# First batch of a fused attention and gated feed-forward kernel: q/k loaded in runs of six tokens, values after the scores, alternating accumulators, and a reordered last normalization

## The chip, the cores and the metric

The kernel runs on one core of a Trainium2 chip. The metric is the device time of one execution in microseconds (us); lower is better. The first runs of the kernel before spread from 421.1 to 425.4 us, and part of the study is about why. The core has a matmul engine (PE in the profile; PEld are its weight loads), a vector engine (DVE), an activation engine (ACT), a pool engine (POOL, which here also issues most loads) and a sync engine (SP) that issues stores and transposing loads.

## The reference, cut to what matters

```python
# q, k, v: (8 batches, 8 heads, 576 tokens, 64), beacon_k/v: (8, 8, 16, 64), all float32
k_all = concat([beacon_k, k]); v_all = concat([beacon_v, v])      # 592 keys
scores = q @ k_all.T / 8;  causal mask on the 576 own keys
a = softmax(scores);  x = (a @ v_all) -> (4608 tokens, 512)
out = (gelu(x @ w_gate) * (x @ w_val)) @ w_out                    # d_ff = 1536
```

## The kernel before: the parts that the change touches

Heads are handled in four pairs per batch. For a pair, q and k are brought into the form "head dimension by token" (`qkT`), four chunks of scores are computed and put through exp, the value matmuls accumulate x and the sum z of the exponentials in PSUM, and the pair is normalized into `xT_sb`. After a batch's four pairs comes the gate/value stage (12 tiles, `gate_val`), whose output matmuls are spread over the next batch's attention. Batches 0 and 1 transpose q/k on the matmul engine, the later ones by DMA.

```python
    def load_perm(src, dst, b, h0, h1):          # batches 0 and 1: runs of 4 tokens (1 KB)
        dma(dst[:, 0:4, ...], src[b, h0:h1, 0:512, :].rearrange("h (p r) d -> p h (r d)", r=4))
        dma(dst[0:64, 4, h0:h1, :], src[b, h0:h1, 512:576, :].rearrange("h p d -> p h d"))
    ...
    def transpose_pe(b, m, pool, tag):           # 19 transposes a pair, then 4 copies on DVE
        ...
    def normalize(b, m):
        x_ps = x_of.pop(i)                       # one tile holds x and z
        act(x_sb, x_ps[:, X0 : X0 + S], ACT.Copy)
        keep(nc.vector.transpose(zT_sb, x_ps[:, Z0 : Z0 + S]))
        keep(nc.vector.reciprocal(r_sb, ...))
        keep(nc.vector.transpose(rec_sb, r_sb broadcast))
        keep(nc.vector.tensor_tensor(out=xT_sb[...], in0=x_sb, in1=rec_sb, op=ALU.mult))
    ...
    def gate_val(ci, fi, kk_late=False):         # kk_late: the matmuls that need the last pair come last
    ...
    load_qk(0)                                   # q, k of pair 0, then of the other pairs: 9 issues
    make_identity(nc, ident)                     # on the pool engine, behind those issues
    ...
    transpose_pe(0, 0, psum_s, "s")
    transpose_pe(0, 1, psum_s, "s")
    ...
        if b == 0:
            ab(0); transpose_pe(0, 2, psum_x, "x"); cd(0); transpose_pe(0, 3, psum_x, "x")
            ab(1); cd(1); ab(2); av(0); cd(2); ab(3); av(1); cd(3); av(2); av(3)
```

`ab` and `cd` are the two halves of a pair's scores, `av` its value matmuls with the normalization. (The last lines are joined here; each call stands on its own line in the kernel.) The kernel keeps every engine's instructions in program order (`keep_in_program_order`).

The softmax here doesn't subtract the row's maximum and nothing guards it: scores larger than these inputs give would overflow.

## Time and profile before

| | us |
|---|---|
| median of the first three runs | 423.2 (421.14 to 425.43) |
| span of the profiled execution | 421.2 |
| gate/value stage of batch 0 runs gapless from | 43.09 |
| one later batch, period | 43.86 |

The page of the kernel before: busy time and share of each engine, then the busy tenths of the matmul engine in 40 slices of 10.5 us.

```profile
PE 384.6 (91%) x2935; PEld 184.2 (44%) x2984; DVE 198.3 (47%) x327; ACT 207.7 (49%) x284; POOL 161.3 (38%) x282
...
PE   2476999999999999999999999999999999999996
```

The matmul engine is the busy one, and the first four slices are where it is not busy. The chain of waits (the work that ended last; columns: start, duration, what) names what holds up those slices. Kernel before, first 45 us:

```profile
6.10 7.80 DMA k_sb_93<-in_k_dram
...
13.94 0.93 PE t_ps L163 x10
...
15.45 1.03 ACT expT L155
...
33.87 0.80 DVE zT_sb L272
...
40.34 0.80 DVE zT_sb L272
...
42.28 0.77 DVE xT_sb L282
```

Scores start late because pair 1's k lands only at 13.9 us; later the chain runs through normalizations. The timeline of the matmul engine shows the idle (columns: start, duration, engine, line, operation, output and inputs, shapes, count; in brackets the idle before it and what ended it). Kernel before:

```profile
8.26 0.80 PE L163 MATMUL t_ps<-ident,q_sb_92 128*64 128x128 bf16 x9 [8.26 <-POOL ident masks.py:199]
...
34.71 0.44 PE L152 MATMUL x_ps<-expT,v_sb_94 128*64 128x496 bf16 x4 [1.17 <-DVE zT_sb L272]
...
37.94 0.44 PE L152 MATMUL x_ps<-expT,v_sb_94 128*64 128x496 bf16 x4 [1.60 <-DVE zT_sb L272]
...
43.09 0.47 PE L152 MATMUL gv_ps<-xT_sb,wg_sb 128*128 128x512 bf16 x1 [2.11 <-DVE xT_sb L282]
...
137.17 0.38 PE L152 MATMUL gv_ps<-xT_sb,wg_sb 128*128 128x512 bf16 x1 [0.61 <-DVE xT_sb L282]
```

Four things wait: the first transposes for the identity, the value steps for the only accumulator, the first gate tile for the last normalization of batch 0, and, in the last line, the first gate tile of a later batch for its last normalization. That last wait stands in each of batches 1 to 7 (0.60 or 0.61 us). The chain of waits of the kernel before just ahead of it:

```profile
133.75 0.66 ACT x_sb L155
...
134.43 0.79 DVE zT_sb L272
...
135.25 0.28 DVE r_sb L274
...
135.55 0.79 DVE rec_sb L277
...
136.36 0.77 DVE xT_sb L282
```

The copy of x (activation engine) and the transpose of z (vector engine) both read the same PSUM tile, one after the other. In this trace the two are never seen at the same time on this tile: in each of the 32 normalizations the transpose starts 0.03 us after the copy ends, and the profile names the copy as what ended its wait (here the copy ends at 134.40, the transpose starts at 134.43).

Last, the clock of the matmul engine. Columns of the stretches view: stretch, length, busy time and count per engine, then the granted clock (1.00 is full), the DMA share and GB/s. Kernel before:

```profile
42.00:44.00 2.00, 0.92 (x3) 0.40 (x3) 1.00 (x2) 0.00 (x0) 0.46 (x1) 0.81 1.25 209
44.00:46.00 2.00, 2.00 (x6) 0.70 (x5) 0.69 (x1) 0.60 (x1) 0.00 (x0) 0.50 1.28 201
46.00:48.00 2.00, 2.00 (x9) 0.80 (x8) 0.24 (x1) 0.60 (x1) 0.00 (x0) 0.84 2.22 160
```

After the 2.11 us of idle the clock is at half for 3.4 us: (1 - 0.81 + 1 - 0.50 + 1 - 0.84) x 2 / 0.5. The gate matmuls of 512 columns start 0.427 us apart in it and 0.216 us apart behind it, so eight of them take 1.7 us more.

### The profile page before, as it was taken

What the parts mean: (1) busy time and instruction counts of PE and PEld (TensorE: products, weight loads), DVE (VectorE), ACT (ScalarE), POOL (GpSimd) and SP (SyncE); (2) the same over time, 40 slices, a digit from 0 to 9 for tenths busy, and PEclk for the clock granted to TensorE, in tenths of its full rate; (3) what the DMA queues carried; (4) which work ended last, traced back from release to release, by engine and by line L of the source; (5) the groups of instructions that cost most, each with busy time, mean ns of one, the idle gap of its engine ahead of it and who ended that gap; (6) DMA issues with size and microseconds to landing.
All of it is one profiled execution on the core that took longest, in us unless ns stands there. A gap on an engine that the chain in (4) does not pass through costs nothing.

```text
span 421.2 us, 7280 instructions
## 1 busy us (share of the span) xinstructions
PE 384.6 (91%) x2935; PEld 184.2 (44%) x2984; DVE 198.3 (47%) x327; ACT 207.7 (49%) x284; POOL 161.3 (38%) x282
## 2 busy tenths in 40 slices
PE   2476999999999999999999999999999999999996
PEld 1244344444444444544454444444444444444442
DVE  0448364474337443654275426642664347443331
ACT  1365225853486338733774378436843585332210
POOL 8825481477046903591249224941410141000000
PEclk9999899999999999999999999999999999999999
DMA  7999990189914991199109941995015010000012
GB/s 82 172 206 197 173 136 3 51 74 164 100 51 48 153 137 50 31 150 159 53 26 129 143 65 51 109 160 70 26 63 89 14 51 32 21 2 25 26 50 100
DMA packets 142289, 36.23 MB, mean 86 GB/s; under 512 B 128944, under 2 KB 137648, under 8 KB 142256
## 3 DMA queue, kind: packets, MB, share of 16 engines
q0 software_dynamic: 107120, 19.15, 60.0%
q1 hardware_dynamic: 35136, 16.62, 18.8%
q8 instruction: 23, 0.38, 0.4%
q14 instruction: 10, 0.08, 0.1%
HBM read 38.27 MB, written 9.44 MB: 113 GB/s over the span
## 4 chain that ended last, share of the span: by engine, by line
PE 80%; ACT 6%; DVE 6%; issue 4%; DMA 2%; POOL 1%; ACTq 0%; POOLq 0%
PE gv_ps L152 42%; PE o_ps L152 19%; PE x_ps L152 9%; PE s_ps L152 7%; ACT expT L155 3%; ACT x_sb L155 3%; PE t_ps L163 2%; DVE zT_sb L272 2%; DMA k_sb_93<-in_k_dram 2%; DVE rec_sb L277 1%; DVE xT_sb L282 1%; POOL q_sb_92 L109 1%; DVE r_sb L274 1%; POOL k_sb_93 L109 0%; DVE qkT L178 0%
## 5 line engine op out<-in xcount | busy, mean ns | idle before, releaser
L155 ACT ACTIVATE ge_sb<-gv_ps 128x512 bf16<-128x512 f32 x108 | 64.5, 597 | 145.6 <-PE gv_ps L152 144.5
L310 DVE TENSOR_TENSOR hT_sb<-gv_ps,ge_sb 128x512 bf16<-128x512 f32 x108 | 74.7, 692 | 118.2 <-ACT ge_sb L155 118.2
L152 PE MATMUL gv_ps<-xT_sb,wg_sb 128*128 128x512 bf16 x428 | 112.8, 382 | 6.7 <-DVE xT_sb L282 6.3
L155 ACT ACTIVATE expT<-s_ps 128x1024 bf16<-128x1024 f32 (+3 forms) x128 | 103.5, 862 | 27.6 <-PE s_ps L152 25.7
L228 POOL TENSOR_SCALAR_AFFINE_SELECT expT<-expT 128x256 bf16<-128x256 bf16 (+2 forms) x140 | 53.6, 392 | 165.0 <-ACT expT L155 164.9
L152 PE MATMUL gv_ps<-xT_sb,wv_sb 128*128 128x512 bf16 x417 | 110.9, 381 | 0.7
L152 PE MATMUL o_ps<-wo_sb,hT_sb 128*128 128x512 bf16 x402 | 103.1, 380 | 3.1 <-issue 2.2
L152 PEld LDWEIGHTS <-wv_sb 128*128 128x128 bf16 x432 | 42.5, 98 | 59.2 <-issue 9.7
L152 PEld LDWEIGHTS <-wg_sb 128*128 128x128 bf16 x432 | 42.1, 98 | 50.6 <-issue 1.2
L152 PEld LDWEIGHTS <-hT_sb 128*128 128x128 bf16 x432 | 37.1, 98 | 47.3 <-issue 9.4
L152 PE MATMUL s_ps<-qkT 64*128 64x80 bf16 (+5 forms) x384 | 39.5, 294 | 6.9 <-ACT expT L155 6.6
L334 DVE COPY o_sb<-o_ps 128x512 f32<-128x512 f32 x36 | 24.8, 689 | 42.5 <-PE o_ps L152 42.5
L152 PE MATMUL x_ps<-expT,ones 128*64 128x144 bf16 (+5 forms) x576 | 43.4, 247 | 0.0
L272 DVE STREAM_TRANSPOSE zT_sb<-x_ps 128x576 f32<-128x576 f32 x32 | 25.1, 783 | 37.3 <-ACT x_sb L155 37.1
L155 ACT ACTIVATE x_sb<-x_ps 128x576 f32<-128x576 f32 x32 | 20.8, 651 | 24.9 <-issue 10.8
L152 PEld LDWEIGHTS <-qkT 64*128 64x128 bf16 x384 | 13.9, 96 | 35.4 <-issue 31.8
L152 PE MATMUL x_ps<-expT,v_sb_94 128*64 128x80 bf16 (+5 forms) x288 | 23.8, 253 | 2.9 <-DVE zT_sb L272 2.8
L282 DVE TENSOR_TENSOR xT_sb<-x_sb,rec_sb 128x576 bf16<-128x576 f32 x32 | 25.1, 784 | 1.1
L152 PEld LDWEIGHTS <-ones 128*64 128x64 bf16 (+1 forms) x576 | 23.4, 112 | 4.9 <-issue 0.2
L277 DVE STREAM_TRANSPOSE rec_sb<-r_sb 128x576 f32<-128x576 f32 x32 | 24.9, 778 | 1.1
L152 PE MATMUL x_ps<-expT,v_sb_97 128*64 128x80 bf16 (+5 forms) x288 | 22.8, 246 | 0.1
L109 POOL DMA_DIRECT2D v_sb_97<-in_v_dram x20 | 17.0, 885 | 7.6 <-DMA k_sb_96<-in_k_dram 3.8
(39 smaller groups left out, 184.4 us busy)
## 6 DMA issues: line engine op xcount, KB each, us to landing
out_dram<-o_sb SPq DMA_DIRECT2D x36, 256.0 KB, 2.0
q_sb_92<-in_q_dram POOLq DMA_DIRECT2D x13, 128.0 KB, 4.3
v_sb_94<-in_v_dram POOLq DMA_DIRECT2D x12, 128.0 KB, 7.6
wg_sb<-in_moe_w_gate_dram POOLq DMA_DIRECT2D x3, 512.0 KB, 10.6
wv_sb<-in_moe_w_val_dram POOLq DMA_DIRECT2D x3, 512.0 KB, 12.4
wo_sb<-in_moe_w_out_dram POOLq DMA_DIRECT2D x1, 1536.0 KB, 18.7
v_sb_97<-in_v_dram POOLq DMA_DIRECT2D x12, 128.0 KB, 9.8
q_sb_95<-in_q_dram POOLq DMA_DIRECT2D x12, 128.0 KB, 4.3
```

The source lines that it names most:

```text
L109: keep(nc.gpsimd.dma_start(out=out_ap, in_=in_ap))
L152: keep(nc.tensor.matmul(out_ap, lhsT, rhs, start=start, stop=stop, **kw))
L155: keep(nc.scalar.activation(out_ap, in_ap, func, **kw))
L163: keep(nc.tensor.transpose(out_ap, in_ap, ident[r0 : r0 + n, r0 : r0 + n]))
L228: nc.gpsimd.affine_select(out=d, in_=d, pattern=[[0, 2], [1, n]], compare_op=ALU.is_ge, fill=0.0, base=NB if t == 0 else 0, channel_multip ...
L272: keep(nc.vector.transpose(zT_sb, x_ps[:, Z0 : Z0 + S]))
L274: keep(nc.vector.reciprocal(r_sb, zT_sb.rearrange("p (c o) -> p c o", o=32)[:, :, 0:1]))
L277: nc.vector.transpose(rec_sb.rearrange("p (c o) -> p c o", o=32), r_sb.to_broadcast([P, S // 32, 32]))
L282: nc.vector.tensor_tensor(out=xT_sb[:, m, b * S : (b + 1) * S], in0=x_sb, in1=rec_sb, op=ALU.mult)
L310: nc.vector.tensor_tensor(out=h_of[ci][:, fi, :], in0=gv_ps[:, 1, :], in1=ge_sb, op=ALU.mult)
L334: keep(nc.vector.tensor_copy(o_sb[:, ti, :], o_ps))
```

## The change

Its intent: start the scores sooner, keep the matmul engine fed in batch 0, and shorten the hand-over to the gate stage. The diff, cut to its core:

```diff
-    def load_perm(src, dst, b, h0, h1): ...
+    def load_qk6(b, h0, h1):                    # runs of 6 tokens, 1.5 KB, no remainder
+        for w, src in enumerate((q, k)):
+            dma(qk6[b][0][0:96, w, h0:h1, :], src[b, h0:h1, :, :].rearrange("h (p r) d -> p h (r d)", r=6))
...
     def transpose_pe(b, m, pool, tag):          # 25 transposes a pair (24 of 96 columns), 2 copies
...
     def attend(b, m, t, wide=False):
+            if wide:                            # x and z in two score buffers instead of the x tile
...
     def normalize(b, m, by_act=False):
+        if by_act:                              # 1/z = exp(-ln z) on ACT, copy of x on DVE
+            act(ln_sb, z_ps, ACT.Ln)
+            keep(nc.vector.tensor_copy(x_sb, x_ps))
+            act(rec_sb, ln_sb, ACT.Exp, scale=-1.0)
+        else:
+            if m == NPAIR - 1:
+                z_first()                       # transpose of z ahead of the copy of x
+            act(x_sb, x_ps, ACT.Copy)
+            if m < NPAIR - 1:
+                z_first()
...
-    load_qk(0)
-    make_identity(nc, ident)
+    load_qk6(0, 0, 2)
+    by_diagonal(ident, ALU.not_equal, 1.0)      # identity after two issues
+    load_kb(0)
+    load_qk6(0, 2, H)
...
         if b == 0:
-            ab(0) T(2) cd(0) T(3) ab(1) cd(1) ab(2) av(0) cd(2) ab(3) av(1) cd(3) av(2) av(3)
+            ab(0) T(1) cd(0) ab(1) T(2) cd(1) ab(2) T(3) cd(2) ab(3) av(0) cd(3)
+            av(1, by_act=True)  av(2, wide=True)  av(3, by_act=True)
```

(The order lines are joined and `transpose_pe(0, n, ...)` is written T(n).) The exp buffers go from three to four. `z_first` for the last pair applies to every later batch; in batch 0 the last pair uses `by_act`.

More of the change, by code (lines that the diff above doesn't have):

```diff
@@ L6 @@
 from concourse._compat import with_exitstack
-from concourse.masks import make_identity
 P = 128
@@ L71 @@
     ring = ctx.enter_context(tc.tile_pool(name="ring", bufs=1))
-    epool = ctx.enter_context(tc.tile_pool(name="epool", bufs=3))
+    epool = ctx.enter_context(tc.tile_pool(name="epool", bufs=4))
     npool = ctx.enter_context(tc.tile_pool(name="npool", bufs=2))
@@ L81 @@
     ident = const.tile([P, P], BF16, name="ident", tag="ident")
+    nc.vector.memset(ident, 0.0)
     ones = const.tile([P, D], BF16, name="ones", tag="ones")
@@ L109, in dma, with load_kb @@
         keep(nc.gpsimd.dma_start(out=out_ap, in_=in_ap))
-    def load_perm(src, dst, b, h0, h1):
-        dma(
-            dst[:, 0:4, :, :].rearrange("p r h d -> p (r h d)").rearrange("p (h x) -> p h x", h=H)[:, h0:h1, :],
-            src[b, h0:h1, 0:512, :].rearrange("h (p r) d -> p h (r d)", r=4),
-        )
-        dma(dst[0:64, 4, h0:h1, :], src[b, h0:h1, 512:576, :].rearrange("h p d -> p h d"))
+    qk6 = {}
+    def load_qk6(b, h0, h1):
+        if b not in qk6:
+            qk6[b] = (
+                hpool.tile([P, 2, H, 6 * D], BF16, name="qk6", tag="hT_sb"),
+                npool.tile([NB, H, D], BF16, name="kb", tag="kb"),
+            )
+        for w, src in enumerate((q, k)):
+            dma(
+                qk6[b][0][0:96, w, h0:h1, :],
+                src[b, h0:h1, :, :].rearrange("h (p r) d -> p h (r d)", r=6),
+            )
+    def load_kb(b):
+        dma(qk6[b][1], beacon_k[b].rearrange("h t d -> t h d"))
     def load_keys(src, beacon, dst, b):
@@ L127, in load_qk @@
         q_sb, k_sb = q_ring[b % NRING], k_ring[b % NRING]
-        if b < NPERM:
-            for h0, h1 in ((0, 2), (2, H)) if b == 0 else ((0, H),):
-                load_perm(q, q_sb, b, h0, h1)
-                load_perm(k, k_sb, b, h0, h1)
-                if h0 == 0:
-                    dma(k_sb[64:80, 4, :, :], beacon_k[b].rearrange("h t d -> t h d"))
-        else:
-            for j in range(4):
-                dma(q_sb[:, j, :, :], q[b, :, j * P : (j + 1) * P, :].rearrange("h p d -> p h d"))
-            dma(q_sb[0:64, 4, :, :], q[b, :, 512:576, :].rearrange("h p d -> p h d"))
-            load_keys(k, beacon_k, k_sb, b)
+        for j in range(4):
+            dma(q_sb[:, j, :, :], q[b, :, j * P : (j + 1) * P, :].rearrange("h p d -> p h d"))
+        dma(q_sb[0:64, 4, :, :], q[b, :, 512:576, :].rearrange("h p d -> p h d"))
+        load_keys(k, beacon_k, k_sb, b)
     def load_v(b):
@@ L158, in transpose_pe, with tr @@
     def transpose_pe(b, m, pool, tag):
-        t_ps = pool.tile([P, 2, 1024 if tag == "s" else 1536], BF16, name="t_ps", tag=tag)
-        def tr(out_ap, in_ap, r0=0):
+        t_ps = pool.tile([P, 3 if tag == "x" else 2, 1024], BF16, name="t_ps", tag=tag)
+        qk, kb = qk6[b]
+        def tr(out_ap, in_ap):
             n = in_ap.shape[0]
-            keep(nc.tensor.transpose(out_ap, in_ap, ident[r0 : r0 + n, r0 : r0 + n]))
-        for w, src in enumerate((q_ring[b % NRING], k_ring[b % NRING])):
-            by_head = src[:, 0:4, :, :].rearrange("p r h d -> p (r h d)").rearrange(
-                "p (h r d) -> p h r d", h=H, r=4
-            )
-            base = 0 if tag == "s" else 512 * w
-            for r in range(4):
-                c = slice(r * P, (r + 1) * P)
-                for hi in range(2):
-                    tr(t_ps[64 * hi : 64 * hi + 64, w, c], by_head[:, 2 * m + hi, r, :])
-            tr(t_ps[:, w, 512:576], src[0:64, 4, 2 * m : 2 * m + 2, :])
-        tr(t_ps[:, 1, 576:592], k_ring[b % NRING][64:80, 4, 2 * m : 2 * m + 2, :], 64)
-        for w in range(2):
-            keep(
-                nc.vector.tensor_copy(
-                    qkT[:, m, w, NB : NB + 512].rearrange("p (t r) -> p t r", r=4),
-                    t_ps[:, w, 0:512].rearrange("p (r t) -> p t r", r=4),
-                )
-            )
-        keep(nc.vector.tensor_copy(qkT[:, m, :, NB + 512 : SK], t_ps[:, :, 512:576]))
-        keep(nc.vector.tensor_copy(qkT[:, m, 1, 0:NB], t_ps[:, 1, 576:592]))
+            keep(nc.tensor.transpose(out_ap, in_ap, ident[0:n, 0:n]))
+        for w in range(2):
+            for r in range(6):
+                for hi in range(2):
+                    tr(
+                        t_ps[64 * hi : 64 * hi + 64, w, r * 96 : (r + 1) * 96],
+                        qk[0:96, w, 2 * m + hi, r * D : (r + 1) * D],
+                    )
+        tr(t_ps[:, 1, S:SK], kb[:, 2 * m : 2 * m + 2, :])
+        keep(
+            nc.vector.tensor_copy(
+                qkT[:, m, :, NB:SK].rearrange("p w (t r) -> p w t r", r=6),
+                t_ps[:, 0:2, 0:S].rearrange("p w (r t) -> p w t r", r=6),
+            )
+        )
+        keep(nc.vector.tensor_copy(qkT[:, m, 1, 0:NB], t_ps[:, 1, S:SK]))
     def transpose_dma(b):
@@ L239, with attend @@
     x_of = {}
-    def attend(b, m, t):
+    def attend(b, m, t, wide=False):
         i = b * NPAIR + m
         if t == AV_ORDER[0]:
-            x_of[i] = psum_x.tile([P, 1536], FP32, name="x_ps", tag="x")
-        x_ps, expT, v_sb = x_of[i], exp_of[i], v_ring[b % NRING]
+            if wide:
+                x_of[i] = tuple(
+                    (psum_s.tile([P, 1024], FP32, name=name, tag="s"), 0, 512) for name in ("xs_ps", "zs_ps")
+                )
+            else:
+                x_ps = psum_x.tile([P, 1536], FP32, name="x_ps", tag="x")
+                x_of[i] = ((x_ps, X0, 512 - X0), (x_ps, Z0, 1024 - Z0))
+        expT, v_sb = exp_of[i], v_ring[b % NRING]
         kr, first, last = KROWS[t], t == AV_ORDER[0], t == AV_ORDER[-1]
-        for base, split in ((X0, 496), (Z0, 432)):
+        for w, (ps, base, split) in enumerate(x_of[i]):
             for q0, q1 in ((S_LO[t], split), (max(split, S_LO[t]), S)):
@@ L253, in attend @@
                     mm(
-                        x_ps[64 * hi : 64 * hi + 64, base + q0 : base + q1],
-                        v_sb[0:kr, t, 2 * m + hi, :] if base == X0 else ones[0:kr, :],
+                        ps[64 * hi : 64 * hi + 64, base + q0 : base + q1],
+                        ones[0:kr, :] if w else v_sb[0:kr, t, 2 * m + hi, :],
                         expT[0:kr, hi, e0 : e0 + q1 - q0],
-                        first and not (base == Z0 and q0 == 0),
+                        first and (wide or not (w == 1 and q0 == 0)),
                         last,
@@ L260, in attend, with normalize, z_first @@
                     )
-    def normalize(b, m):
+    def normalize(b, m, by_act=False):
         i = b * NPAIR + m
-        x_ps = x_of.pop(i)
+        (x_ps, xc, _), (z_ps, zc, _) = x_of.pop(i)
+        x_ps, z_ps = x_ps[:, xc : xc + S], z_ps[:, zc : zc + S]
         del exp_of[i]
         x_sb = npool.tile([P, S], FP32, name="x_sb", tag="x_sb")
-        act(x_sb, x_ps[:, X0 : X0 + S], ACT.Copy)
-        zT_sb = npool.tile([P, S], FP32, name="zT_sb", tag="zT_sb")
-        keep(nc.vector.transpose(zT_sb, x_ps[:, Z0 : Z0 + S]))
-        r_sb = npool.tile([P, S // 32, 1], FP32, name="r_sb", tag="r_sb")
-        keep(nc.vector.reciprocal(r_sb, zT_sb.rearrange("p (c o) -> p c o", o=32)[:, :, 0:1]))
-        rec_sb = npool.tile([P, S], FP32, name="rec_sb", tag="rec_sb")
-        keep(
-            nc.vector.transpose(
-                rec_sb.rearrange("p (c o) -> p c o", o=32), r_sb.to_broadcast([P, S // 32, 32])
+        rec_sb = npool.tile([P, S], FP32, name="rec_sb", tag="rec_sb")
+        if by_act:
+            ln_sb = npool.tile([P, S], FP32, name="ln_sb", tag="zT_sb")
+            act(ln_sb, z_ps, ACT.Ln)
+            keep(nc.vector.tensor_copy(x_sb, x_ps))
+            act(rec_sb, ln_sb, ACT.Exp, scale=-1.0)
+        else:
+            zT_sb = npool.tile([P, S], FP32, name="zT_sb", tag="zT_sb")
+            r_sb = npool.tile([P, S // 32, 1], FP32, name="r_sb", tag="r_sb")
+            def z_first():
+                keep(nc.vector.transpose(zT_sb, z_ps))
+            if m == NPAIR - 1:
[3 more added lines that the diff above has]
+                z_first()
+            keep(nc.vector.reciprocal(r_sb, zT_sb.rearrange("p (c o) -> p c o", o=32)[:, :, 0:1]))
+            keep(
+                nc.vector.transpose(
+                    rec_sb.rearrange("p (c o) -> p c o", o=32), r_sb.to_broadcast([P, S // 32, 32])
+                )
             )
-        )
         keep(
@@ L336, in out_mms, with by_diagonal @@
                 keep(nc.sync.dma_start(out=out[n0 : n0 + P, :], in_=o_sb[:, ti, :]))
-    load_qk(0)
-    make_identity(nc, ident)
-    keep(
-        nc.gpsimd.affine_select(
-            out=tri,
-            in_=tri,
-            pattern=[[1, P]],
-            compare_op=ALU.is_ge,
-            fill=0.0,
-            base=0,
-            channel_multiplier=-1,
-        )
-    )
+    def by_diagonal(tile_, op, fill):
+        keep(
+            nc.gpsimd.affine_select(
+                out=tile_, in_=tile_, pattern=[[1, P]], compare_op=op, fill=fill, base=0, channel_multiplier=-1
+            )
+        )
+    load_qk6(0, 0, 2)
+    by_diagonal(ident, ALU.not_equal, 1.0)
+    load_kb(0)
+    load_qk6(0, 2, H)
+    by_diagonal(tri, ALU.is_ge, 0.0)
     load_v(0)
@@ L354 @@
         load_gate_val(i)
-    load_qk(1)
+    load_qk6(1, 0, H)
+    load_kb(1)
     load_out_w()
@@ L358 @@
     transpose_pe(0, 0, psum_s, "s")
-    transpose_pe(0, 1, psum_s, "s")
     for b in range(B):
@@ L374, in cd, with av @@
             scores(b, m, 3)
-        def av(m):
+        def av(m, wide=False, by_act=False):
             for t in AV_ORDER:
-                attend(b, m, t)
-            normalize(b, m)
+                attend(b, m, t, wide)
+            normalize(b, m, by_act)
         keep(nc.scalar.preload_act_table_set(SET_EXP))
@@ L383 @@
             ab(0)
+            transpose_pe(0, 1, psum_x, "x")
+            cd(0)
+            ab(1)
             transpose_pe(0, 2, psum_x, "x")
-            cd(0)
-            transpose_pe(0, 3, psum_x, "x")
-            ab(1)
             cd(1)
             ab(2)
-            av(0)
+            transpose_pe(0, 3, psum_x, "x")
             cd(2)
             ab(3)
-            av(1)
+            av(0)
             cd(3)
-            av(2)
-            av(3)
+            av(1, by_act=True)
+            av(2, wide=True)
+            av(3, by_act=True)
         else:
```

## The prediction

> **What bounds it now.** Page, busy shares: the matmul engine is busy 91% of the 421.2 us span; the timeline shows it nearly gapless from 46.7 us on. Two kinds of time are not matmul-bound.
>
> 1. The first 43 us. The chain of waits runs: first q/k issues, identity ready only at 8.26 us (after all nine q/k issues), the rest of batch 0's k landed at 13.94, first exp at 15.45, then matmul idle of 0.99, 1.17, 1.60 and 2.11 us, ended by exp, by the zT transpose freeing the only x accumulator, and by the last normalization. The gate/value stage runs gapless only from 43.09. Matmuls are slow for most of this stretch: 512-column ones start 0.42 us apart until 46.5 and 0.216 later. [...] the granted clock of 0.50 in 44 to 46 us agrees.
> 2. At the start of the gate/value stage of batches 1 to 7 the matmul engine idles 0.61 us for xT (seven times). The chain: x_sb copy 0.66, zT 0.80, r 0.28, rec 0.79, multiply 0.77 us.
>
> **Removed, added, moved.**
> - Identity after two q/k issues: ready about 3.1 us. First pair's q/k landed near 5.5 to 6, its transposes done near 7, copies (about 1.5 us, from 0.64 us per 512 columns) by 8.5; first exp near 9 instead of 15.45.
> - The rest of q/k is issued about 2.4 us sooner in half as many pieces; it should land near 11.3, not 13.94. That gates pair 1's transposes and takes back half of the gain at the first exp. From there about 4.5 us a pair (scores, transposes 1.7, copy 1.5, queued behind the masks of exp). All but the last half-pair's scores are done near 23.5 to 24.
> - Then value matmuls for four pairs: 2.9 us each at the slow clock, 1.6 fast (both in the trace). Pair 2 has its own accumulators, pairs 1 and 3 free theirs after about 1.3 us (Ln 0.65, copy 0.65). The idle of 1.17 and 1.60 mostly goes. I expect the fast clock during pair 1. The vector queue (pair 2's 2.6 us chain, then pair 3's copy and multiply) ends last: xT of pair 3 near 36.6 us, against 43.09. Gain 6.5 us.
> - If the clock stays fast over this hand-over, the slow start of the gate stage goes too (eight matmuls at +0.21 = 1.7 us). I count 1.1.
> - For the last pair of every later batch zT now precedes the x_sb copy: 0.66 off the chain, more than the 0.61 idle. Seven times 0.6 = 4.2 us, all on the critical path.
> - Batch 1's transposes: 25 instead of 19 a pair, but 96 columns, not 128: about 1.06 us as before. Weight loads and later loads have slack.
>
> **Time.** 423.2 - 6.5 - 1.1 - 4.2 = 411.4; call it 411.5 us, range 408 to 415. Faster by over 2% (under 414.7): 0.85; within 2%: 0.14; slower: 0.01.
>
> **What would show it.** First exp near 9 us; pair 1's k transposes near 11.3; last idle before the gate stage ending near 36.6, the granted clock not falling to 0.5 after it; no idle of 0.6 us ended by xT in later batches; batch 1's transposes still about 1.06 us each inside the gate stage.
>
> **What would make it wrong.** The rest of k landing at 13 (value loads now follow at once): 1.7 lost. Matmuls slow to the end of the stage: 2 lost. Half clock again at the hand-over: 1 lost. Fast clock from the scores on: 2 gained. Transposing z first could delay the activation table load behind the x copy. Copies with a stride of six could be slower.

## The result, and the profile after

The changed kernel takes 410.49 us (median of four runs, 410.28 to 410.67) against 423.11 for the kernel before: ratio 0.970, 95% interval 0.965 to 0.975. A ratio is the mean time of one kernel's runs over that of the other's runs of the same rounds, so it is not quite the ratio of the medians. Executions over 1.5% slower than the fastest of the same kernel are left out of the means. The prediction was 411.5 us in a range of 408 to 415.

The page of the changed kernel, the lines that answer to those shown of before (slices of 10.2 us here):

```profile
PE 385.3 (94%) x3036; PEld 183.0 (45%) x3036; DVE 194.7 (48%) x308; ACT 209.2 (51%) x286; POOL 156.3 (38%) x275
...
PE   2678999999999999999999999999999999999996
```

The matmul work is the same (385.3 us busy against 384.6); the span shrank around it. The chain of waits of the changed kernel, first 45 us:

```profile
4.37 7.50 DMA qk_103<-in_k_dram
...
11.91 0.81 PE t_ps L167 x9
...
13.26 0.95 ACT expT L158
...
27.71 0.79 DVE zT_sb L289
...
35.19 0.68 DVE x_sb L282
...
35.96 0.77 DVE xT_sb L303
```

The rest of k is still what the chain goes through first, but it lands 2.0 us sooner (11.91 against 13.94). The timeline of the matmul engine, changed kernel:

```profile
4.77 1.40 PE L167 MATMUL t_ps<-ident,qk_103 96*64 96x96 bf16 x24 [4.77 <-DMA qk_103<-in_q_dram]
...
28.55 0.43 PE L155 MATMUL x_ps<-expT,v_sb_95 128*64 128x496 bf16 x4 [1.01 <-DVE zT_sb L289]
...
35.24 0.38 PE L155 MATMUL gv_ps<-xT_sb,wg_sb 128*128 128x512 bf16 x1 [1.37 <-DVE xT_sb L303]
...
36.77 0.38 PE L155 MATMUL gv_ps<-xT_sb,wg_sb 128*128 128x512 bf16 x1 [0.51 <-DVE xT_sb L303]
```

The first transposes wait for data, not for the identity. One wait for an accumulator is left of two, and the gate stage is gapless from 36.77 instead of 43.09 us. Idle of 0.6 us at the start of a later batch's gate stage no longer exists. Its timeline in batch 2 of the changed kernel (all engines, cut):

```profile
124.42 0.78 DVE L289 STREAM_TRANSPOSE zT_sb<-x_ps 128x576 f32<-128x576 f32 x1
125.23 0.27 DVE L296 RECIPROCAL r_sb<-zT_sb 128x18 f32<-128x18 f32 x1
125.29 0.65 ACT L158 ACTIVATE x_sb<-x_ps 128x576 f32<-128x576 f32 x1 [2.26 <-DVE zT_sb L289]
...
125.96 1.28 ACT L441 ACT_TABLE_LOAD   x1
...
126.42 0.76 DVE L303 TENSOR_TENSOR xT_sb<-x_sb,rec_sb 128x576 bf16<-128x576 f32 x1
...
127.23 0.38 PE L155 MATMUL gv_ps<-xT_sb,wg_sb 128*128 128x512 bf16 x1
```

The last line carries no bracket: xT is ready (126.42 + 0.76 = 127.18) when the matmul engine comes to it. The copy of x now waits for z and runs beside the reciprocal, off the chain; the table load ends at 127.24, before the first gelu needs it (127.86). The period of a later batch falls from 43.86 to 43.29 us.

The clock at the new hand-over, changed kernel:

```profile
36.00:38.00 2.00, 1.49 (x8) 0.58 (x6) 0.71 (x1) 0.69 (x2) 0.64 (x1) 1.00 1.26 206
38.00:40.00 2.00, 2.00 (x11) 0.88 (x9) 0.94 (x2) 0.60 (x1) 1.61 (x2) 1.00 1.25 209
```

It stays full. Finally batch 1's transposes inside the gate stage (tile view of `t_ps`; nanoseconds min/median/max, first and last start). Before:

```profile
L163 PE MATMUL t_ps<-ident,k_sb_96 x40: 178/219/243, 56.1 to 65.3; 128*64 128x128 bf16 x32, 64*128 64x64 bf16 x4, 16*128 16x16 bf16 x4
```

After:

```profile
L167 PE MATMUL t_ps<-ident,qk_126 x96: 206/206/231, 47.6 to 56.4; 96*64 96x96 bf16 x96
```

Single durations hide the throughput, since these matmuls overlap (a transpose of 206 ns is followed by another after 4 or 38 ns); a set's cost is read from its place in the timeline of the matmul engine. Before:

```profile
55.65 0.55 PE L163 MATMUL t_ps<-ident,q_sb_95 128*64 128x128 bf16 x9
56.13 0.66 PE L163 MATMUL t_ps<-ident,k_sb_96 128*64 128x128 bf16 x10
56.72 1.04 PE L152 MATMUL gv_ps<-xT_sb,wg_sb 128*128 128x512 bf16 x4
```

After:

```profile
47.65 0.70 PE L167 MATMUL t_ps<-ident,qk_126 96*64 96x96 bf16 x24
48.28 0.18 PE L167 MATMUL t_ps<-ident,kb 16*128 16x16 bf16 x1
48.39 1.04 PE L155 MATMUL gv_ps<-xT_sb,wg_sb 128*128 128x512 bf16 x4
```

A pair's set took 1.07 us before (55.65 to 56.72) and takes 0.74 us now (47.65 to 48.39). Two of the four sets now start 0.25 us later than the other two, behind a wait for the copy.

The single start times in the trace, which these views merge, show where the 0.33 us went. Two transposes of 64 columns that fill the two halves of the output partitions start 4 ns apart, as a couple. With 128 columns a couple follows the last one after 56 ns, with 96 columns after 42.5 ns. So the twelve couples of now take longer than the eight of before (0.51 against 0.45 us). What is gone are the two transposes of the remaining 64 tokens, which write all 128 partitions at once: each of them started 0.15 us after the last couple, and the next transposes 0.13 us after it, so that each added about 0.23 us. The beacon's transpose now bears such a pause itself (0.10 us more than before). The gain thus comes from loads without a remainder, not from shorter transposes; this is read from the two traces, and no run separates it.

The 12.8 us between the two profiled spans (421.18 - 408.39) add up as follows.

| term | predicted | profiled pair |
|---|---|---|
| gate stage of batch 0 starts (43.09 to 36.77) | 6.5 | 6.3 |
| full clock after it | 1.1 | 1.7 |
| batch 1's transposes | 0 | 0.8 |
| seven later gate stages | 4.2 | 4.0 |
| sum | 11.8 | 12.8 |

The stretch from the gate stage's start to the first wait of batch 1's scores shrank by 2.48 us (36.13 to 33.65). The start times split it. The first ten gate matmuls take 3.84 us before (half clock) and 2.15 after, so 1.69 is the clock; the transposes give the rest, 0.79: four sets at 0.32 less two delays of 0.25. The clock's 1.7 belongs to this pair of profiles, of which one fell to half clock and the other did not.

### The profile page after: what moved, and what is told of

Same layout as the page of the kernel before. It is cut to its first block, busy times and chain, and to the rows that moved or that the text cites. A ratio compares the mean times of both kernels' runs of the same rounds, so it can differ in the third digit from the quotient of the medians.

```text
span 408.4 us, 7414 instructions
## 1 busy us (share of the span) xinstructions
PE 385.3 (94%) x3036; PEld 183.0 (45%) x3036; DVE 194.7 (48%) x308; ACT 209.2 (51%) x286; POOL 156.3 (38%) x275
## 4 chain that ended last, share of the span: by engine, by line
PE 88%; ACT 4%; DVE 4%; DMA 2%; issue 1%; POOL 1%; POOLq 0%; DVEq 0%
PE gv_ps L155 45%; PE o_ps L155 23%; PE x_ps L155 12%; PE s_ps L155 7%; ACT expT L158 3%; DMA qk_103<-in_k_dram 2%; ACT x_sb L158 1%; DVE qkT L178 1%; PE t_ps L167 1%; DVE xT_sb L303 1%; POOL qk_103 L109 0%; DVE zT_sb L289 0%; DVE x_sb L282 0%; DVE hT_sb L331 0%; ACT ge_sb L158 0%
## 5 line engine op out<-in xcount | busy, mean ns | idle before, releaser
L155 PE MATMUL gv_ps<-xT_sb,wv_sb 128*128 128x512 bf16 x432 | 112.2, 379 | 0.0
L155 PE MATMUL o_ps<-wo_sb,hT_sb 128*128 128x512 bf16 x432 | 107.3, 381 | 0.0
L355 DVE COPY o_sb<-o_ps 128x512 f32<-128x512 f32 x36 | 24.8, 689 | 42.5 <-PE o_ps L155 42.5
L155 PE MATMUL x_ps<-expT,ones 128*64 128x432 bf16 (+1 forms) x558 | 42.1, 247 | 0.0
L289 DVE STREAM_TRANSPOSE zT_sb<-x_ps 128x576 f32<-128x576 f32 x29 | 22.7, 781 | 32.4 <-ACT x_sb L158 32.4
L158 ACT ACTIVATE x_sb<-x_ps 128x576 f32<-128x576 f32 x29 | 18.9, 651 | 27.4 <-DVE zT_sb L289 15.8
L155 PEld LDWEIGHTS <-qkT 64*128 64x128 bf16 x384 | 13.8, 96 | 37.2 <-issue 27.3
L298 DVE STREAM_TRANSPOSE rec_sb<-r_sb 128x576 f32<-128x576 f32 x30 | 23.3, 778 | 1.0
L155 PE MATMUL x_ps<-expT,v_sb_95 128*64 128x80 bf16 (+5 forms) x270 | 22.4, 253 | 1.1 <-DVE zT_sb L289 1.0
L155 PE MATMUL x_ps<-expT,v_sb_98 128*64 128x80 bf16 (+5 forms) x288 | 22.8, 246 | 0.1
```

The source lines that it names most:

```text
L155: keep(nc.tensor.matmul(out_ap, lhsT, rhs, start=start, stop=stop, **kw))
L158: keep(nc.scalar.activation(out_ap, in_ap, func, **kw))
L289: keep(nc.vector.transpose(zT_sb, z_ps))
L298: nc.vector.transpose(rec_sb.rearrange("p (c o) -> p c o", o=32), r_sb.to_broadcast([P, S // 32, 32]))
L355: keep(nc.vector.tensor_copy(o_sb[:, ti, :], o_ps))
```

## The experiments

Each run was correct. Each was timed together with the kernel before on the same chip, over three rounds (e1 to e8) or five. "Clock" is the mean granted clock of one run. A value of 0.994 to 0.996 is read as one window of 3.4 us at half clock, which is an estimate: the profile of the kernel before shows one such window and a mean of 0.996, and half of 3.4 over its span of 421 is 0.004. Values of 0.998 and more are too high for such a window; the profiles of both kernels have a short half-clock tail behind the last matmul (1.30 and 1.21 us). The split is used below (a run with such a window "fell"), and it was made after the runs were seen.

### e1: z first, alone

```diff
     # kernel before
-        act(x_sb, x_ps[:, X0 : X0 + S], ACT.Copy)
+        if m < NPAIR - 1:
+            act(x_sb, x_ps[:, X0 : X0 + S], ACT.Copy)
         keep(nc.vector.transpose(zT_sb, x_ps[:, Z0 : Z0 + S]))
+        if m == NPAIR - 1:
+            act(x_sb, x_ps[:, X0 : X0 + S], ACT.Copy)
```

> Kernel before, with nothing changed but that the last pair of every batch transposes z ahead of the copy of x. Theory (the copy of 0.66 us lies on the chain that the matmul engine waits for at each gate/value start): the seven idles of 0.61 us in batches 1 to 7 vanish (4.2 us) and batch 0's chain shortens by 0.66: 423.1 goes to about 418.3, and the batch period seen in the timeline falls from 43.86 to 43.3 us. Rival (the activation table load, now behind a later copy, hands the time back): the idle goes but exp/gelu start later, and the time stays above 421.

Measured: 416.8 us (416.5 to 417.5) against 423.3, ratio 0.984 (0.980 to 0.988). The seven idles are gone, the batch period is 43.29 (one batch 43.99), and the hand-over idle in batch 0 is 1.54 instead of 2.11 us. The gain is 6.5 rather than the expected 4.9 us. All four runs have a clock of 0.998 or more, so none fell, where the kernel before fell in 19 of 36 runs (below); that the shorter idle is the reason is not shown. The rival (table load) is out.

### e2: the changed kernel with x first again

```diff
-            if m == NPAIR - 1:
-                z_first()
             act(x_sb, x_ps, ACT.Copy)
-            if m < NPAIR - 1:
-                z_first()
+            z_first()
```

> Changed kernel with the copy of x put back ahead of z in the last pair of batches 1 to 7 (batch 0's last pair uses the other normalization and is not touched). Theory: the seven idles of 0.6 us come back: 410.5 goes to about 414.7, the gate stage of batch 0 still starting at 36.8 us. Rival (the later batches gained from something else, such as the fourth exp buffer): stays within 1 us of 410.5.

Measured: 415.0 us (413.9 to 417.5). The gate stage of batch 0 starts at 36.68 us, as in the changed kernel (36.77), and seven idles of 0.60 or 0.61 us are back. The slowest run had a clock of 0.996, and its matmul engine also waited 1.34 us for a transposing load in a later batch (at 196.56 us), so that its excess is not the clock's alone; the other three average 414.65, which is 4.1 us above the changed kernel. The fourth exp buffer is not the reason for the later batches' gain.

### e3: the loads, the early identity and the new transposes, alone

The edit is the changed kernel with the order of batch 0, the single accumulator, three exp buffers and x first as in before.

```diff
+    transpose_pe(0, 1, psum_s, "s")
...
-            ab(0) T(1) cd(0) ab(1) T(2) cd(1) ab(2) T(3) cd(2) ab(3) av(0) cd(3) av(1, by_act=True) ...
+            ab(0) T(2) cd(0) T(3) ab(1) cd(1) ab(2) av(0) cd(2) ab(3) av(1) cd(3) av(2) av(3)
```

> The new q/k loads, early identity and new transposes alone; order of batch 0, one accumulator, three exp buffers and x ahead of z as in before. Theory (the old order transposes pair 1 before the first scores, so the first exp is gated by the rest of k, which lands near 11.9 instead of 13.94): everything in batch 0 shifts by about 2.1 us and no more: about 421, first exp near 13.3, last idle before the gate stage ends near 41. Rival (the load is the larger part of the start's gain of 6.3 us): 419 or less.

Measured: 418.8 us (417.7 to 421.3), ratio 0.988. The profiled run is the slow one of the four, 421.3 us, with k at 11.96 and the gate stage at 41.90 us. It shows the clock fall:

```profile
42.00:44.00 2.00, 2.00 (x6) 0.76 (x5) 0.58 (x1) 0.60 (x1) 0.00 (x0) 0.52 1.62 183
44.00:46.00 2.00, 2.00 (x8) 0.69 (x6) 0.11 (x1) 0.06 (x1) 0.99 (x2) 0.62 2.39 155
```

The other three runs (clock 0.999 or 1.0) average 418.4. In the run that fell the loads are worth about what was expected; in the others 3.0 us against the kernel before's own runs without a fall (421.4, below). The expected 421 was thus the value for one clock state only. The 3.0 us hold the new transposes of batch 1 too (0.8), so the earlier start is worth about 2.2, near the 2.1 that were expected. By the median, the rival's threshold of 419 was reached; by comparing like states it was not the larger part of the start.

### e4: order, accumulators and normalizations, alone

The edit is the kernel before with the new order of batch 0, `wide`, `by_act` and four exp buffers; loads and transposes old, x first.

> The new order of batch 0, its alternating accumulators and normalizations and four exp buffers alone; loads, identity and transposes as in before, x ahead of z in later batches. Theory: pair 1's scores wait for k at 13.94 and start near 16.5 (changed kernel 14.26), the rest follows as in the changed kernel, the gate stage starts gapless near 39.1 us and at full clock: 423.1 - 4.0 - 1.7 = 417.4. If the clock falls at the hand-over after all: 419. Rival (without the new loads the order gains nothing): 422 or more.

Measured: the profiled run (461.8 us, clock 0.861) is not used. The three runs are 417.3, 418.4 and 418.8, with a clock of 1.0, against 417.4 expected. The order gains without the loads.

### The clock of the kernel before, over all rounds

The kernel before ran 36 times beside these experiments. 19 runs have a clock of 0.994 to 0.996 and average 423.6 us; 17 have 0.998 or more and average 421.4. That is most of the spread of the kernel before: by the mean clocks, one window at half clock in about half of the runs. The one profile shows it at the hand-over, and 1.7 us for it; what else separates the two groups is not shown. Within the runs that did not fall, the three parts add up: e1 416.9, e3 418.4 and e4 418.2 are 4.5, 3.0 and 3.2 us below 421.4, in sum 10.7, and the changed kernel's nine such runs average 410.6, which is 10.8 below. Compared by medians, the parts seem to give 6.5 + 4.5 + 4.9 = 15.9 us, more than the whole, because each of them alone also has fewer falls (none in four runs of e1, one in four of e3, none in three of e4, against 19 in 36).

### e5: identity late

```diff
     # changed kernel
     load_qk6(0, 0, 2)
-    by_diagonal(ident, ALU.not_equal, 1.0)
     load_kb(0)
...
     # in load_keys, behind the second value load of batch 0
+            if b == 0 and j == 1 and src is v:
+                by_diagonal(ident, ALU.not_equal, 1.0)
```

> Changed kernel with the identity made after two of the value loads, near 7.8 us instead of 3.1 (before: 8.26). Theory (pair 1's scores are gated by the rest of k, landing at 11.9, and by the vector queue): the first exp moves from 8.9 to about 11.9, but the first scores of pair 1 only from 14.26 to about 15.7, and the time by 1.4 us to about 411.9. Rival (the time of the first exp is what counts): the whole 3 us, 413.5.

Measured: 412.3 us (410.8 to 414.5). In the profile the transposes start at 7.71, the first exp at 11.18 (2.3 us later) and pair 1's scores at 15.45 (1.2 us later than 14.26). The gate stage starts at 37.77 instead of 36.77. Two of the four runs fell (0.995, 0.996); the two others are 410.8 and 411.6. So a delay of 3 us in the first transposes costs about 1 us by the gate stage, and 0.6 us by the runs that did not fall (411.2 against the changed kernel's 410.6): the time of the first exp is not what counts.

### e6: pair 1's q/k in issues of their own

```diff
     load_kb(0)
-    load_qk6(0, 2, H)
+    load_qk6(0, 2, 4)
+    load_qk6(0, 4, H)
```

> Changed kernel with pair 1's q/k in two issues of their own ahead of the other four heads' (two issues of 0.7 us more). Theory: pair 1's k lands near 9 instead of 11.9, its transposes follow pair 0's scores at once, its scores start near 12.9 instead of 14.26, and the whole is 1.4 us faster, about 409.1. Rival (the loads are bound by bytes, and further issues only delay them): 410.5 or more.

Measured: 410.44 us (408.5 to 411.5), where 409.1 was expected: a miss by the median. But two of the four runs fell (0.995, 0.996); the other two, 410.68 and 408.48, average 409.6, which is 1.0 us below the changed kernel's like runs. So part of the gain may be there; two runs are few. The profile is of the slower of the two. The timeline of the matmul engine, e6:

```profile
12.60 1.01 PE L155 MATMUL s_ps<-qkT 64*128 64x512 bf16 x8 [1.46 <-DVE qkT L183]
...
26.89 0.69 PE L155 MATMUL x_ps<-expT,v_sb 128*64 128x496 bf16 x4 [0.89 <-DVE zT_sb L289]
...
36.47 0.38 PE L155 MATMUL gv_ps<-xT_sb,wg_sb 128*128 128x512 bf16 x1 [0.51 <-DVE xT_sb L303]
```

Pair 1's scores start 1.66 us sooner than in the changed kernel and its value step too (26.89 against 28.55), as expected. But the group of four 496-column matmuls takes 0.69 us there instead of 0.43: the engine is still at half clock. The first clock record of this trace stands at 30.7 us, that of the changed kernel's at 27.3. Of the 1.66 us, 0.3 reach the gate stage in this execution. The release of the clock itself moves from one execution to the next: the changed kernel's second profile has its first record at 25.84 us and the gate stage from 36.17, 0.6 us sooner than the first profile.

### e7: one accumulator

```diff
-            av(1, by_act=True)
-            av(2, wide=True)
-            av(3, by_act=True)
+            av(1)
+            av(2)
+            av(3)
```

> Changed kernel with only the one x accumulator and the old normalization (z ahead of x in the last pair) in batch 0; order and loads kept. Theory: pairs 2 and 3 wait again about 1.5 us each for the copy and zT, the last chain is 2.7 us instead of the present vector queue, so xT of pair 3 is ready near 39 instead of 36.7: about 412.9; 414.6 or more if the longer idle at the hand-over lets the clock fall. Rival (moving the value steps behind the scores is what gains, the accumulators hide nothing): within 0.7 us of 410.5.

Measured: 413.62 us (412.7 to 414.8), ratio to before 0.978. The waits for zT are back (1.17, 1.56 and 1.61 us), and the gate stage is gapless from 38.69 us. No run fell. The accumulators with their normalizations are worth about 3 us, so the order alone is not all that gains.

### e8: the kernel before with its hand-over idle filled

```diff
         for n, (w, kk) in enumerate(order):
+            if filler and n == 6:               # batch 0, first gate tile: 9 matmuls nobody reads
+                f_ps = psum_o.tile([P, D_MODEL], FP32, name="f_ps", tag="o")
+                for _ in range(filler):
+                    mm(f_ps, wg_sb[:, 0, 0:P], xT_sb[:, 0, 0:CH], True, True)
```

> Kernel before with nine idle-filling matmuls of 512 columns, whose result nobody reads, in the 2.1 us before the gate stage of batch 0. Theory (that idle lets the clock fall to half for one window, which costs the first eight gate matmuls 1.7 us): the gate stage still starts near 43.1, its matmuls start 0.216 us apart at once, the granted clock stays 1.0 in 44 to 46 us, and the time falls by 1.7 to 2.5 us, to about 421.3. Rival (the clock falls for another reason, or the filler runs late): 423 or more, clock 0.5 in 44 to 46.

Measured: 421.39 us (420.6 to 423.0), ratio 0.996 (0.992 to 1.000), clock 0.999 or 1.0 in all four runs, while 5 of the 7 runs of the kernel before beside it fell. The time is that of the kernel before's runs without a fall (421.4). With the idle filled no run fell; four runs against seven are few. In its profile the clock reads 1.00 from 42 to 48 us, and the gate matmuls start 0.21 to 0.22 us apart (44.63, 44.84, 45.06). (In the profiled run the gate stage starts at 44.6, not 43.1: the second value step still ran at the slow pace, with 0.69 us for four 496-column matmuls at 31.81 against 0.44 at 31.52 in the kernel before, so that the value stage itself was longer.)

### The changed kernel again

> The changed kernel itself, again. The kernels e2, e5 and e6 share its hand-over to the gate stage (idles of about 1.4 and 0.5 us), and 5 of their 12 runs show a clock of 0.995 or 0.996 (one window at half clock), but none of the changed kernel's own four runs did. If that was chance, some of these runs show 0.996 and are about 2 us longer (412 to 413); if the changed kernel's timing avoids it, all show 1.0 and 410.5.

Measured: 410.53 us (409.9 to 412.2; five rounds), ratio 0.973 (0.970 to 0.977). One run of six shows 0.995 and is the longest (412.2); another of 412.0 shows 1.0, so not every long run has fallen. With the first four runs that is one fall in ten, and five in twelve for e2, e5 and e6, whose hand-over is alike. So the change seems to make the fall rarer but does not exclude it.

What decides a single run is not shown. The profiles of the kernel before and of the changed kernel hold this much of it. In the kernel before, a record of full clock runs from 29.58 to 43.24 us, one of half clock from 43.24 to 46.65 (3.41 us), and the next one of full clock lasts 375.47 us. In the 3.41 us ahead of the fall the matmul engine was busy for 38%; in the 3.41 us ahead of the rises (at 29.58 and 46.65, and at 27.27 in the changed kernel) it was busy all the time. The profile of the changed kernel holds no fall from 27.27 us to the last matmul.

How much idle brings a fall is not shown. With 2.11 us ahead of the gate stage (the kernel before) 19 of 36 runs fell; with two idles, 1.37 and 0.51 us in the changed kernel and similar ones in e2, e5 and e6, 6 of 22; with 1.54 us (e1) none of four. In all, the kernel before fell in 19 of 36 runs, the changed kernel, e2 and e5 in 4 of 18, e3 in one of four, e6 in two of four, and e1, e7, e8 and e11 in none of their 18.

### e9: the changed kernel with its idle filled

```diff
+    def fill(n):
+        for _ in range(n):
+            mm(fill_ps, fill_sb[:, 0:P], fill_sb, True, True)     # nobody reads fill_ps
...
+    fill(8)                                     # before the first transposes, while q/k are loaded
     transpose_pe(0, 0, psum_s, "s")
+    fill(5)
...                                              # 4, 5, 5 in the waits of the score steps, 3 before av(1),
                                                 # 5 before the last chunk of the first gate tile
```

> Changed kernel with matmuls that nobody reads filling the idle of the matmul engine from 1.3 us on: before the first transposes, in the waits between the score steps, before the second value step and before the last chunk of the first gate tile. Theory (the matmul engine stays at half clock until about 27 us only because it idles some 1.5 us in each score step of 4.4 us; half clock costs there mainly the first value step, 2.9 instead of 1.6 us, and luck of the window at the hand-over): full clock by about 8 us, first value step 1.6 us, the gate stage starts near 35 instead of 36.8, all clocks 1.0, about 408.7. Rival (the release comes at its time whatever the engine does, or the fillers stand in the way of real work): 410.5 or more.

Measured: 409.08 us (408.5 to 409.9), against 410.53 for the changed kernel. The first clock record stands at 10.6 us instead of 27, the second value step starts at 26.21 instead of 28.55, and the gate stage is gapless from 34.84, as expected (35). The mean clock is below 0.997 in five of six runs (0.991 to 0.996) although their times are short. Ahead of the first record a profile can read 1.00 at the slow pace: in the kernel before the clock reads 1.00 from 26 to 28 us, where four 496-column matmuls take 0.69 us, and the first record is at 29.58. So an early release followed by a fall among the score steps may look like the runs of e9; this is a guess. No trace of such a run was taken, so this stays open.

### e10: a version that combines what the runs pointed to

The edit is e9 with e6's loads, and two changes on the vector engine: the causal masks of batch 0 are queued behind the next pair's copy of transposes, and pairs 2 and 3 are normalized by Ln and Exp and multiplied straight out of the accumulator.

```diff
-                keep(nc.vector.tensor_tensor(out=d, in0=d, in1=w, op=ALU.min))
+                pending.append((d, w))          # issued by masks(), after transpose_pe(0, m + 1)
...
-            keep(nc.vector.tensor_copy(x_sb, x_ps))
+            if m == 1:
+                keep(nc.vector.tensor_copy(x_sb, x_ps))
+            else:
+                x_sb = x_ps
...
-            av(2, wide=True)
+            av(2, wide=True, by_act=True)
```

> e9's fillers, e6's separate issue of pair 1, the masks of batch 0 queued behind the next pair's copy on the vector engine, and pairs 1 to 3 normalized by Ln and Exp with pairs 2 and 3 multiplied straight from the accumulator. Theory (with clock, load and vector queue out of the way the score stage is bound by exp alone, 3.4 us a pair instead of 4.4, and the last chain is Ln, Exp, multiply, 2.1 us after the last value matmul): gate stage from about 30 us instead of 36.8, total about 404. Rival (the gains overlap, as they did in e6, or the weights' or batch 1's loads then hold up the gate stage): 407 or more.

Measured: 404.06 us (403.8 to 405.0), ratio 0.9575 (0.954 to 0.961) to the kernel before, all clocks 0.999 or 1.0. The end of the hand-over in its timeline of the matmul engine:

```profile
29.25 1.24 PE L157 MATMUL fill_ps<-fill_sb 128*128 128x512 bf16 x5
30.33 0.38 PE L157 MATMUL gv_ps<-xT_sb,wg_sb 128*128 128x512 bf16 x1
```

The gate stage is gapless from 30.33 us, 6.4 us sooner than in the changed kernel, and the total is 6.5 us lower. Nothing after that point takes the gain back.

### e11: e10 without the filling matmuls

```diff
     def fill(n):
-        for _ in range(n):
+        for _ in range(0):
```

> e10 with its filling matmuls taken out and nothing else. In e6 the earlier load moved all score steps 1.66 us ahead, but the full clock came only at 30.7 us, the second value step ran at half clock, and the gate stage started only 0.3 us sooner. Theory (load and vector queue gains reach the end only if the matmul engine is at full clock by the value steps): the clock is released only near 25 to 28 us, the gate stage starts near 33 instead of 30.3, and the time is about 406.5, with some runs another 2 us longer by a fall at the hand-over. Rival (the fillers add nothing once the vector queue is short): 404 to 404.7.

Measured: 406.05 us (405.1 to 407.2), ratio 0.962. Timeline of the matmul engine:

```profile
19.57 1.01 PE L157 MATMUL s_ps<-qkT 64*128 64x512 bf16 x8 [0.83 <-ACT expT L160]
...
25.05 0.44 PE L157 MATMUL x_ps<-expT,v_sb 128*64 128x496 bf16 x4 [1.14 <-DVE zT_sb L306]
...
32.09 0.38 PE L157 MATMUL gv_ps<-xT_sb,wg_sb 128*128 128x512 bf16 x1 [0.63 <-DVE xT_sb L320]
```

The first clock record is at 23.5 us, at the end of the first value step, and the gate stage starts at 32.09. Up to there the matmul engine idles 0.83 us in each score step of 3.77 us, and the value step takes 2.9 us without a gap. With the gaps filled the first record stands at 10.6 (e9) and 5.0 us (e10). The load and vector-queue edits are worth about 4.5 us without the fillers, and the fillers 2.0 us on top (e10 and e11: their ratios to the kernel before, 0.9575 and 0.9623, give the same 2.0). No run fell here, which was not expected; the hand-over has a single idle of 0.63 us.

## Why the prediction was right

The predicted time was 411.5 us, and 410.5 was measured twice. Part of the close agreement is luck. Without the clock, the terms predicted a gain of 10.7 us, and the runs that did not fall show 10.8 (421.4 to 410.6); but in that sum the start and the later batches gave 0.2 us less each than predicted, and the transposes 0.8 that were not predicted. Point by point:

- **The start.** The chain of waits was read correctly. Predicted and measured in the changed kernel's profile: identity-bound transposes gone (first transposes at 4.77), first exp at 9 and 8.90, rest of k at 11.3 and 11.91, a score step of 4.5 and 4.4 us, last hand-over idle ending at 36.6 and 36.77. e5 confirms the step that mattered most in this sum: the gain at the first exp (6.5 us) does not pass through, since the rest of k (2.0 us sooner) and the copies of each score step gate what follows. e7 confirms the accumulators.
- **z first.** 4.2 us were predicted; the batch period gives 7 x 0.57 = 4.0, undoing it costs 4.1 (e2), and doing it alone gains it (e1). The named risk, the table load, did not come true: it ends at 127.24 us, and gelu starts at 127.86 in the profile shown.
- **The clock at the hand-over.** 1.1 us were counted, a guess between 0 and 1.7. In the profiled pair it was 1.7, the whole of it, because one profile fell and the other did not. Over many runs it is a matter of odds: the kernel before fell in 19 of 36 runs, the changed kernel in one of ten, and the runs that fell are about 2.3 us longer (423.6 against 421.4). e8 (no fall in four runs with the idle filled) points to the idle as its cause. The prediction treated the clock as something that the kernel's own schedule decides; e2, e5 and e6 (five falls in twelve runs, with the same hand-over) show it as something that the schedule makes more or less likely; why one run falls and another does not is not shown.
- **Full clock in the value stage.** "During pair 1" was right for this trace: the first clock record is at 27.3 us, the second value step starts at 28.55 and takes 1.64 us, where the first took 2.93.
- **The mis-sized term** is the one written as "about 1.06 us as before" for batch 1's transposes. A set takes 0.74 us against 1.07, so this term gave 0.8 us and not zero. The count of instructions went up by a third, and the time went down by 0.33 us a pair. The prediction had scaled one measured rate per transpose, but in the set of 19 the time was not spread evenly: two transposes of the 64-token remainder took about 0.23 us each, and the new loads leave no remainder.

What stays open: how much idle brings a fall, the low mean clocks of e9, why a change between couples and full-width transposes brings a pause (0.15 and 0.13 us), and the part of the 2.3 us that the half-clock window's 1.7 us does not cover.

## What to carry to other kernels

At the start of a kernel, ask of every gain what the next gate is: here a first exp 6.5 us sooner did not pass through (undoing 2.3 us of it cost about 1, e5), because another load and an in-order vector queue came next. Look once at every hand-over from one stage to the next, in every iteration: moving one 0.65 us copy off the chain was worth a third of this change. And before explaining a spread of one per cent, split the runs by granted clock: here an idle of 2.11 us ahead of dense matmuls went with a window of 3.41 us at half clock in about half of the runs, parts measured alone each claimed that same window, and idle filled with matmuls that nobody reads was a cheap remedy (no fall in four runs of e8; 2.0 us between e11 and e10). When repeated small instructions change their shape, look for what a remainder costs before counting instructions.
